# Expert results turned by VectorE and scattered as quarter rows, in an attention and mixture-of-experts kernel

## The chip, the cores and the metric

The kernel runs on one core of a Trainium2 chip, as one launch. The metric is the device time of one execution in microseconds. Engines are named as in the profile: PE (TensorE), PEld (its weight loads), DVE (VectorE), ACT (ScalarE), POOL (GpSimd) and SP (the queue that issues most DMAs).

## The reference

Two layers. The first is a gated linear attention over 4 batches, 8 heads, 768 steps and 48 columns per head. Its output, 3072 tokens of 384 columns, goes through a mixture of 8 experts, of which each token uses the one with the highest logit:

```python
f = 1.0 / (1.0 + np.exp(-f_logit))
for t in range(S):
    state = f[:, :, t, :, None] * state + np.einsum('bhd,bhe->bhde', k[:, :, t], v[:, :, t])
    y[:, :, t] = np.einsum('bhd,bhde->bhe', q[:, :, t], state)
x = y.transpose(0, 2, 1, 3).reshape(B * S, H * D)             # 3072 x 384
e_idx = np.argmax(x @ w_gate, axis=1)
gate_w = softmax(x @ w_gate)[np.arange(N), e_idx]
eom = 1.0 / (1.0 + np.exp(-(x @ w_output_gate)))
for e in range(E):                                             # 8 experts
    mask = e_idx == e
    ye = np.maximum(x[mask] @ w1[e], 0.0) @ w2[e]              # 384 -> 1024 -> 384
    out[mask] = gate_w[mask, None] * eom[mask, e, None] * ye
```

## The kernel before

**Attention and routing.** The attention works in 24 chunks of 128 tokens. Each chunk's rows, with 384 columns, the token's number and 2 x 8 logits behind them (`RW` = 401 numbers), are scattered by POOL into `xs_dram`, where each expert has its own slots. These scatters are declared independent of each other.

**The experts in order of size.** `Experts.run` goes through the stages s = 0 to 7. The largest expert comes first, and stage s makes room for `CAPS[s]` tokens: 512, 448, 432, 416, 400, 400, 384, 376. A stage has two halves. The first product (`mm1`, eight steps f of nine matmuls, L782) gives h, with columns for tokens; ACT and DVE split it into a high and a low part (`hh` L786, `hl` L787). The second product (`mm2`, eight steps of nine matmuls, L804) gives y in three PSUM tiles of 128 columns of the model each. Every operand is split into a high and a low part, so that each product is three matmuls. Stage 0 does half of its work early, while the last attention chunk ends.

**What runs beside PE.** In the first half `split` makes the high (ACT, L657) and low (DVE, L658) parts of w2. In the second half the list `front` holds, for the next expert, the four splits of w1 and three `x_in` (a DVE turn L743, an ACT cast L749, a DVE subtraction L750); one of them is taken at each step f. In stage 0 the three `x_in` come ahead of the remaining splits. The gain operations (`gain_ops`, 13 of them on DVE, ACT and POOL, L719 to L733) make each token's factor `k.gain` and its row number `k.dst`; up to two are taken at each step, for the next expert, in the second half.

**How results leave.** For experts of over 384 slots (s = 0 to 5) `y_out` copies the three PSUM tiles to SBUF at the end of the stage (L829). In the next stage, at steps f = 1 to 4 of the first product, `put` turns 128 tokens at a time back with three PE transposes (L835), ACT scales them (L838) and POOL scatters 128 rows of 384 columns to `out` (L843). The two smallest experts (s = 6, 7) use `mm2_rows` (L818), which gives rows directly.

**Order.** `chain` fixes each of DVE, ACT, POOL and PE to the order in which the program writes its instructions. SP issues DMAs in program order as well: `load` issues w1 of the next expert, `load_rest` its tokens (`tokens_in`, four loads L686 of 32 partitions and one, L690, of the 17 numbers behind each row, 68 B) and then w2 (L647). `load(1)` and `load_rest(1)` stand at the beginning of `run`, ahead of stage 0's second product. `first_m` holds these numbers for s = 0; it is loaded in two parts with that expert's early and late tokens.

Of the kernel before, what the change touches and what calls it, by code (L numbers as in the profile page):

```python
# [26 lines left out]
TS = 128  # L27
# [12 lines left out]
QW = KC * BL  # L40
NTC = N // C
# [7 lines left out]
HELD = 256  # L49

# [546 lines left out]
class Experts:  # L597
# [4 lines left out]
    def __init__(self, tc, nc, k, r, raw, right, w1, w2, xs_dram, out, kp):  # L602
        self.tc, self.nc, self.k, self.r, self.raw, self.right, self.kp = tc, nc, k, r, raw, right, kp
        self.w1, self.w2, self.xs, self.out = w1, w2, xs_dram.rearrange("(e n) w -> e n w", e=E), out
        k.gain = kp.tile([TS, NT, E], F32, name="gain")
        k.dst = kp.tile([TS, NT, E], I32, name="dst")

        self.first = kp.tile([128, SLOTS // BL, QW], F32, name="first_x")
        self.first_m = kp.tile([TS, NT, RW - DM], F32, name="first_m")
        self.apart, self.cleared, self.number = [], [], {}  # L610
        self.wr, self.whl, self.todo, self.gq = {}, {}, [], []
        self.xq, self.xt, self.hs, self.ys, self.ysb = {}, {}, {}, {}, {}
# [11 lines left out]
    def open_rest(self, ctx):  # L624
        pool = lambda name, bufs, **kw: ctx.enter_context(self.tc.tile_pool(name=name, bufs=bufs, **kw))
        self.xp, self.hp, self.yp = pool("mo_x", 2), pool("mo_h", 9), pool("mo_y", 1)
        self.psy, self.pso = pool("mo_psy", 1, space=PSUM), pool("mo_pso", 1, space=PSUM)
        self.yt = [self.yp.tile([128, SLOTS], F32, name=f"y{d}") for d in range(KC)]
# [22 lines left out]
    def split(self, m, s, i, eng=None):  # L651
        flat = lambda a: a.rearrange("p a b -> p (a b)")
# [4 lines left out]
        self.nc.scalar.copy(out=flat(hi), in_=flat(t))  # L657
        (eng or self.nc.vector).tensor_tensor(out=flat(lo), in0=flat(t), in1=flat(hi.bitcast(F32)), op=ALU.subtract)  # L658
# [17 lines left out]
    def tokens_in(self, s, j0, j1):  # L676
# [4 lines left out]
        if s == 0:  # L681
            t, m = self.first, self.first_m
        else:
            t, m = (self.xp.tile([128, SLOTS // BL, QW], F32, name="xq"),
                    self.xp.tile([TS, NT, RW - DM], F32, name="xm"))
# [4 lines left out]
        loads.append(self.nc.sync.dma_start(  # L690
            out=m[:, j0:j1, :], in_=self.xs[e, j0 * TS:j1 * TS, DM:RW].rearrange("o (j p) w -> p (o j) w", p=TS)))
# [6 lines left out]
        else:  # L698
            self.meta = getattr(self, "meta", []) + [(s, 0, j1, m)]
        self.xq[s] = t  # L700

    def gains(self):

        kp = self.kp
        for s, j0, j1, t in self.meta:
            n = j1 - j0
            d, up, dn = (kp.tile([128, NT, E], F32, name=m)[:, 0:n] for m in ("g_d", "g_up", "g_dn"))
            mx, sm, so = (kp.tile([128, NT], F32, name=m)[:, 0:n] for m in ("g_mx", "g_sm", "g_so"))
            self.gq += self.gain_ops(s, j0, j1, t, d, up, dn, mx, sm, so)
        self.meta = []  # L710

    def gain_ops(self, s, j0, j1, t, d, up, dn, mx, sm, so):
        nc, k = self.nc, self.k
        tt, red, act = nc.vector.tensor_tensor, nc.vector.tensor_reduce, nc.scalar.activation
        sig, n = AF.Sigmoid, j1 - j0
        lg, og = t[:, 0:n, 1:1 + E], t[:, 0:n, 1 + E:1 + 2 * E]
        mine = k.perm[:, s, :] if s > 0 else self.r.top
        return [
            lambda: nc.gpsimd.tensor_scalar(out=k.dst[:, j0:j1, s], in0=t[:, 0:n, 0], scalar1=0.0,  # L719
                                            scalar2=float(BIG), op0=ALU.max, op1=ALU.min),  # L720
            lambda: red(out=mx, in_=lg, axis=AX.X, op=ALU.max),
            lambda: tt(out=d, in0=lg, in1=mx.unsqueeze(2).broadcast_to([128, n, E]), op=ALU.subtract),

            lambda: (act(out=up, in_=d, func=sig), act(out=dn, in_=d, func=sig, scale=-1.0)),
            lambda: tt(out=d, in0=og, in1=mine.unsqueeze(1).broadcast_to([128, n, E]), op=ALU.mult),
            lambda: red(out=so, in_=d, axis=AX.X, op=ALU.add),
            lambda: act(out=so, in_=so, func=sig),
            lambda: nc.vector.reciprocal(out=dn, in_=dn),
            lambda: tt(out=up, in0=up, in1=dn, op=ALU.mult),
            lambda: red(out=sm, in_=up, axis=AX.X, op=ALU.add),  # L730
            lambda: nc.vector.tensor_scalar(out=sm, in0=sm, scalar1=1e-9, scalar2=None, op0=ALU.add),
            lambda: nc.vector.reciprocal(out=sm, in_=sm),
            lambda: tt(out=k.gain[:, j0:j1, s], in0=sm, in1=so, op=ALU.mult),  # L733
# [60 lines left out]
    def mm2(self, s, f, part=0):  # L794
# [4 lines left out]
        for d in range(KC):  # L799
            if f == 0 and part == 0:  # L800
                self.ys[d] = self.psy.tile([128, 512], F32, name=f"y_ps{d}")
            ds = slice(d * 128, d * 128 + 128)
            for i, (a, b) in enumerate(((wh, hh), (wl, hh), (wh, hl))):
                self.nc.tensor.matmul(self.ys[d][:, c0:c0 + n], a[:, f % 2, ds], b,  # L804
# [3 lines left out]
    def mm2_rows(self, s, step):  # L808

        k, nc = self.k, self.nc  # L810
        for j, n in self.rows(s):
            ps = self.psy.tile([128, 512], F32, name=f"y_ps{j}")
# [11 lines left out]

    def y_out(self, s):
        for d in range(KC):
            t = self.yt[d]
            copy = self.nc.vector.tensor_copy if d == 1 else self.nc.scalar.copy
            copy(out=t[:, 0:CAPS[s]], in_=self.ys[d][:, 0:CAPS[s]])  # L829
            self.ysb[s, d] = t  # L830

    def put(self, s, j, n):
        ps = self.pso.tile([128, KC, 128], F32, name="o_ps")
        for d in range(KC):
            self.nc.tensor.transpose(out=ps[:, d, :], in_=self.ysb[s, d][:, j * TS:j * TS + TS],  # L835
                                     identity=self.k.ident)
        t = self.yp.tile([TS, DM], F32, name="o", bufs=3)
# [316 lines left out]
```

## Time and profile before

| | |
|---|---|
| median of 3 runs | 360.17 us (360.13 to 360.51) |
| profiled execution | 360.28 us |
| its span in the trace | 358.5 us |
| granted clock over the span | 0.998 |

The span runs from the first to the last instruction of the program in the trace; 1.78 us of the profiled execution lie around it. Times below are in microseconds from the span's start, unless they are in ns.

### The profile page before, as it was taken

To read this page: it belongs to the slowest core of one execution; us is meant where nothing else is said; L and a number is where in the kernel's file an instruction comes from. 1 tells how busy PE (TensorE), PEld (TensorE's weight loads), DVE (VectorE), ACT (ScalarE), POOL (GpSimd) and SP (SyncE) were. 2 spreads that over 40 slices of the span, in tenths; PEclk is the share of its full clock that TensorE was granted. 3 is DMA by queue.
4 is the path that set the end of the run, shared out by engine and by line. 5 is a ranking of instruction groups with operands and counts; after the bars stand their busy time and mean duration, and the time that the engine had idled before them with its cause. 6 is when DMAs were issued, how large, how long until landed. Compare 5 with 4: busy or idle time off the path is not lost.

```text
span 358.5 us, 8438 instructions
## 1 busy us (share of the span) xinstructions
PE 346.2 (97%) x3109; PEld 324.2 (90%) x3109; DVE 245.3 (68%) x510; ACT 198.1 (55%) x468; POOL 144.4 (40%) x183
## 2 busy tenths in 40 slices
PE   7899999999999899999999999999999999999992
PEld 2678898988988899999999999999999999999992
DVE  6998989898996775785764774583684584475600
ACT  3476776776766652566535645644654654654510
POOL 8586789899989850002112201210210310232011
PEclk9999999999999999999999999999999999999999
DMA  7999999999527935968674456356555555421001
GB/s 256 350 359 354 346 257 271 295 269 261 197 66 254 284 109 155 278 193 189 190 187 99 159 182 141 135 181 137 180 179 117 181 181 123 169 91 39 0 25 45
DMA packets 66117, 67.11 MB, mean 187 GB/s; under 512 B 22019, under 2 KB 60694, under 8 KB 66065
## 3 DMA queue, kind: packets, MB, share of 16 engines
q1 hardware_dynamic: 62752, 56.82, 57.2%
q0 software_dynamic: 3312, 9.65, 7.4%
q8 instruction: 26, 0.43, 0.5%
q14 instruction: 27, 0.21, 0.2%
HBM read 53.53 MB, written 13.39 MB: 187 GB/s over the span
## 4 chain that ended last, share of the span: by engine, by line
PE 88%; DVE 4%; DMA 3%; ACT 2%; issue 2%; POOL 0%; POOLq 0%; ACTq 0%; DVEq 0%
PE h_ps L782 31%; PE y_ps L804 24%; PE x_ps L336 6%; PE a_ps L248 5%; PE y_ps L818 5%; PE two_ps L316 3%; PE two_ps L308 3%; PE one_ps L316 3%; PE kn_ps L265 3%; PE one_ps L281 2%; PE o_ps L835 2%; DMA out<-o,dst 1%; DVE p L212 1%; DVE i L219 1%; DMA f_t<-in_f 1%
## 5 line engine op out<-in xcount | busy, mean ns | idle before, releaser
L843 POOL DMA_INDIRECT out<-o,dst x30 | 30.5, 1015 | 171.2 <-ACT o L838 97.5
L787 DVE SCALAR_TENSOR_TENSOR hl<-h_ps,hh 128x256 fp32r<-128x256 f32 (+6 forms) x72 | 39.3, 546 | 49.2 <-ACT hh L786 48.9
L782 PE MATMUL h_ps<-xh,w1h 128*128 128x400 f32 (+6 forms) x192 | 67.1, 349 | 0.0
L782 PE MATMUL h_ps<-xh,w1l 128*128 128x400 f32 (+6 forms) x192 | 65.1, 339 | 0.0
L782 PE MATMUL h_ps<-xl,w1h 128*128 128x400 f32 (+6 forms) x192 | 65.0, 339 | 0.0
L786 ACT ACTIVATE hh<-h_ps 128x256 fp32r<-128x256 f32 (+6 forms) x72 | 34.8, 484 | 47.8 <-PE h_ps L782 46.8
L804 PE MATMUL y_ps<-hh,w2h 128*128 128x256 f32 (+4 forms) x168 | 55.7, 332 | 0.0
L804 PE MATMUL y_ps<-hh,w2l 128*128 128x256 f32 (+4 forms) x168 | 55.6, 331 | 0.0
L804 PE MATMUL y_ps<-hl,w2h 128*128 128x256 f32 (+4 forms) x168 | 55.6, 331 | 0.0
L782 PEld LDWEIGHTS h_ps<-xl,w1h 128*128 128x128 f32 x192 | 36.1, 188 | 0.4
L782 PEld LDWEIGHTS h_ps<-xh,w1l 128*128 128x128 f32 x192 | 36.0, 188 | 0.5
L782 PEld LDWEIGHTS h_ps<-xh,w1h 128*128 128x128 f32 x192 | 36.1, 188 | 0.4
L658 DVE TENSOR_TENSOR w2l<-w2r,w2h 128x768 fp32r<-128x768 f32 x31 | 29.7, 958 | 4.2 <-ACT w2h L657 2.0
L226 POOL TENSOR_TENSOR q_t<-q_t,p 128x512 f32<-128x512 f32 x24 | 30.6, 1275 | 4.6 <-DVE p L212 4.4
L804 PEld LDWEIGHTS y_ps<-hh,w2h 128*128 128x128 f32 x168 | 31.6, 188 | 0.4
L804 PEld LDWEIGHTS y_ps<-hl,w2h 128*128 128x128 f32 x168 | 31.6, 188 | 0.4
L804 PEld LDWEIGHTS y_ps<-hh,w2l 128*128 128x128 f32 x168 | 31.6, 188 | 0.4
L212 DVE TENSOR_TENSOR_SCAN p<-f_ps,start_p 128x511 f32<-128x511 f32 x22 | 28.0, 1274 | 3.7 <-ACT start_p L200 2.0
L248 PE MATMUL a_ps<-q_t,k_t 64*128 64x128 f32 x384 | 28.3, 285 | 2.2 <-ACT kn L273 1.4
L658 DVE TENSOR_TENSOR w1l<-w1r,w1h 128x768 fp32r<-128x768 f32 x29 | 27.8, 958 | 3.7 <-ACT w1h L657 3.0
L749 ACT CAST xh<-xr 128x400 fp32r<-128x400 f32 (+6 forms) x24 | 12.2, 518 | 31.7 <-DVE xr L743 31.6
L223 POOL TENSOR_TENSOR k_t<-k_t,i 128x512 f32<-128x512 f32 x21 | 26.9, 1282 | 3.6 <-DVE i L219 2.6
(168 smaller groups left out, 741.8 us busy)
## 6 DMA issues: line engine op xcount, KB each, us to landing
w1r<-in_w SPq DMA_DIRECT2D x32, 384.0 KB, 3.9
w2r<-in_w SPq DMA_DIRECT2D x32, 384.0 KB, 3.2
v_t<-in_v SPq DMA_DIRECT2D x12, 512.0 KB, 9.3
xs_dram<-empty SPq DMA_DIRECT2D x8, 401.0 KB, 10.6
f_t<-in_f SPq DMA_DIRECT2D x6, 512.0 KB
q_t<-in_q SPq DMA_DIRECT2D x6, 512.0 KB
k_t<-in_k SPq DMA_DIRECT2D x6, 512.0 KB, 9.6
f_t<-in_f SPq DMA_DIRECT2D x12, 192.0 KB, 8.7
```

Of the source, the lines that this page charges most:

```text
L212: nc.vector.tensor_tensor_scan(out=flat(d["p"])[:, 1:n], data0=flat(d["f"])[:, 0:n - 1], data1=sp[:, 1:n], initial=sp[:, 0:1], op0=ALU.mul ...
L223: eng.tensor_tensor(out=k_t[i][:, :, sl], in0=k_t[i][:, :, sl], in1=d["i"], op=ALU.mult)
L226: nc.gpsimd.tensor_tensor(out=q_t[i][:, :, sl], in0=q_t[i][:, :, sl], in1=d["p"], op=ALU.mult)
L248: nc.tensor.matmul(aps[t][par][:, g, :], k_t[b % 2][r, g, sl], q_t[b % 2][r, g, sl], start=(g == 0), stop=(g == NP - 1))
L316: nc.tensor.matmul(yps[t][g % 2][r0:r0 + 64, g // 2, :], v_t[b][:, c, 64 * h:64 * h + 64], at[t][:, h % 2, g, :], start=((first or c == 0) ...
L336: nc.tensor.matmul(xps[t][:, g, :], xt[t][:, g, :], turn[:, g, :], start=(g == 0), stop=(g == NP - 1))
L658: (eng or self.nc.vector).tensor_tensor(out=flat(lo), in0=flat(t), in1=flat(hi.bitcast(F32)), op=ALU.subtract)
L782: nc.tensor.matmul(ps[:, 0:n], a[:, c, cs], b, start=(i == 0), stop=(i == 3 * KC - 1))
L786: nc.scalar.activation(out=hi, in_=ps[:, 0:n], func=AF.Relu)
L787: nc.vector.scalar_tensor_tensor(out=lo, in0=ps[:, 0:n], scalar=0.0, in1=hi.bitcast(F32), op0=ALU.max, op1=ALU.subtract)
L804: self.nc.tensor.matmul(self.ys[d][:, c0:c0 + n], a[:, f % 2, ds], b, start=(f == 0 and i == 0 and part == 0), stop=(f == KF - 1 and i == ...
L843: self.nc.gpsimd.indirect_dma_start(out=self.out, out_offset=bass.IndirectOffsetOnAxis(ap=self.k.dst[0:n, j, s:s + 1], axis=0), in_=t[0:n] ...
```

## The change

- `y_out` uses three DVE transposes of 32x32 blocks, straight from PSUM, into a tile with two buffers. Columns of w2 are permuted in `split`, so that after this turn partition 32q + i holds quarter q (96 columns) of token i of a block of 32. The PE transposes, the tile `o_ps` and the copies of y are gone.
- `put` now takes a block of 32 tokens: ACT scales 128x96 in place, and POOL scatters 128 quarter rows. For s = 0 to 5 that is 16, 14, 14, 13, 13 and 13 blocks. They start at step f = 5 of the next stage's first product, two a step, and go on through its second product.
- All scatters to `out` are declared independent of each other.
- The 17 numbers behind each row are loaded by `meta_in`: for s = 0 to 5 in four loads, one to each 32 partitions, so that each quarter row has its own scale and row number. `meta_in(0)` stands at the beginning of `run`, after `load(1)` and ahead of `load_rest(1)`; the others stand after their expert's tokens.
- `gains(s)` runs in stage s: in the first product for s > 0, in the second product for s = 0. It uses Exp in place of Sigmoid, and one ACT operation fewer.
- The count in `check` uses an `h_ps` buffer.

```diff
+TURNED = sum(c > KC * 128 for c in CAPS)
+HOLD = 5
...
+        self.ys = [self.psy.tile([128, 512], F32, name=f"y_ps{d}") for d in range(KC)]
...
     def load_rest(self, s):
             self.tokens_in(s, 0, len(self.rows(s)))
+            self.meta_in(s)
...
     def split(self, m, s, i, eng=None):
+        if m == 2 and s < TURNED:
+            to = lambda a: a.rearrange("p a b -> p (a b)").rearrange("p (c x i) -> p x c i", c=KC, i=BL)
+            of = lambda a: a.rearrange("p a (q c i) -> p (a q) c i", c=KC, i=BL)
...
-        self.nc.scalar.copy(out=flat(hi), in_=flat(t))
+        self.nc.scalar.copy(out=to(hi), in_=of(t))
...
-        loads.append(self.nc.sync.dma_start(
-            out=m[:, j0:j1, :], in_=self.xs[e, j0 * TS:j1 * TS, DM:RW].rearrange("o (j p) w -> p (o j) w", p=TS)))
...
+    def meta_in(self, s):
+        e, nb = bass.ds(self.number[s], 1), self.blocks(s)
+        m = self.xp.tile([128, SLOTS // BL, RW - DM], F32, name="xm")
+        if s < TURNED:
+            for q in range(NQ):
+                self.nc.sync.dma_start(
+                    out=m[BL * q:BL * q + BL, 0:nb, :],
+                    in_=self.xs[e, 0:BL * nb, DM:RW].rearrange("o (a j) w -> j (o a) w", j=BL))
+            self.meta[s] = (nb, m)
...
+            lambda: act(out=up, in_=d, func=AF.Exp),
...
+            lambda: act(out=so, in_=so, func=AF.Exp, scale=-1.0),
...
+    def blocks(self, s):
+        return -(-CAPS[s] // BL)
+
     def y_out(self, s):
+        nb = self.blocks(s)
+        t = self.ysb[s] = self.yp.tile([128, SLOTS // BL, QW], F32, name="yr", bufs=2)
         for d in range(KC):
-            t = self.yt[d]
-            copy = self.nc.vector.tensor_copy if d == 1 else self.nc.scalar.copy
-            copy(out=t[:, 0:CAPS[s]], in_=self.ys[d][:, 0:CAPS[s]])
-            self.ysb[s, d] = t
-
-    def put(self, s, j, n):
-        ps = self.pso.tile([128, KC, 128], F32, name="o_ps")
-        for d in range(KC):
-            self.nc.tensor.transpose(out=ps[:, d, :], in_=self.ysb[s, d][:, j * TS:j * TS + TS],
-                                     identity=self.k.ident)
-        t = self.yp.tile([TS, DM], F32, name="o", bufs=3)
-        self.nc.scalar.activation(out=t[0:n], in_=ps[0:n].rearrange("p a b -> p (a b)"), func=AF.Copy,
-                                  scale=self.k.gain[0:n, j, s:s + 1])
-        self.scatter(s, j, n, t)
+            self.nc.vector.transpose(out=t[:, 0:nb, BL * d:BL * d + BL], in_=self.ys[d][:, 0:BL * nb])
+
+    def put(self, s, a):
+        t = self.ysb[s][:, a, :]
+        self.nc.scalar.activation(out=t, in_=t, func=AF.Copy, scale=self.k.gain[:, a, s:s + 1])
+        self.other_rows(self.nc.gpsimd.indirect_dma_start(
+            out=self.out.rearrange("n (q w) -> (n q) w", q=NQ),
+            out_offset=bass.IndirectOffsetOnAxis(ap=self.k.dst[:, a, s:s + 1], axis=0),
+            in_=t, in_offset=None, bounds_check=NQ * N - 1, oob_is_err=False))
+
+    def other_rows(self, i):
+        for other in self.put_out:
+            self.tc.declare_no_dep(i.ins, other.ins, reason="other tokens")
+        self.put_out.append(i)
...
     def run(self):
         step(len(self.todo))
+        self.meta_in(0)
         self.load_rest(1)
...
-            back = self.rows(s - 1) if s > 0 and len(self.rows(s - 1)) > KC else []
+            back = list(range(self.blocks(s - 1))) if 0 < s <= TURNED else []
...
+            if s > 0:
+                self.gains(s)
             for f in range(KF):
                 self.mm1(s, f)
+                self.gain(2)
...
-                if 1 <= f <= len(back):
-                    self.put(s - 1, *back[f - 1])
+                if s <= TURNED and f >= HOLD:
+                    put(2)
...
+            if s == 0:
+                self.gains(s)
...
                 if front:
                     front.pop(0)()
+                put(2)
                 self.gain(2)
```

## Rows read from the trace of the kernel before

**Rows 1.** The page, part 1: busy us (share of the span) and instructions.

```profile
PE 346.2 (97%) x3109; PEld 324.2 (90%) x3109; DVE 245.3 (68%) x510; ACT 198.1 (55%) x468; POOL 144.4 (40%) x183
```

**Rows 2.** Windows of first products, s = 1 to 6; columns: PE, PEld, DVE, ACT, POOL.

```profile
157.15:173.06 15.91, 15.91 (x85) 14.64 (x85) 9.97 (x18) 9.44 (x17) 2.51 (x2) 1.00 0.77 193
...
sum 89.11, PE 89.11 PEld 85.99 DVE 46.66 ACT 53.93 POOL 17.62; mean PE 14.85 PEld 14.33 DVE 7.78 ACT 8.99 POOL 2.94
```

**Rows 3.** Windows, second products of s = 1 to 6: the first and all six.

```profile
173.06:187.59 14.53, 14.53 (x74) 13.45 (x74) 10.77 (x30) 6.23 (x12) 2.54 (x3) 1.00 0.64 185
...
sum 80.89, PE 80.89 PEld 79.41 DVE 59.33 ACT 36.95 POOL 10.90; mean PE 13.48 PEld 13.24 DVE 9.89 ACT 6.16 POOL 1.82
```

**Rows 4.** Chain of waits: start us, us, what.

```profile
148.70 8.45 PE y_ps L804 x72
157.15 3.71 PE h_ps L782 x18
160.86 0.33 PE o_ps L835 x3
```

**Rows 5.** Groups by line and form: busy us, mean ns, idle before and releaser.

```profile
L843 POOL DMA_INDIRECT out<-o,dst x30 | 30.5, 1015 | 171.2 <-ACT o L838 97.5 <-ACT o L822 27.9 <-ACT hh L786 15.9
...
L838 ACT ACTIVATE o<-o_ps,gain 128x384 f32<-128x384 f32 x19 | 11.0, 581 | 0.0
...
L295 DVE TENSOR_TENSOR misc<-one_ps,state 128x192 f32<-128x192 f32 x16 | 5.8, 361 | 5.3 <-ACT xt L330 5.0
...
L743 DVE STREAM_TRANSPOSE xr<-xq 128x448 f32<-128x448 f32 x6 | 3.8, 635 | 0.3 <-DMA xq<-xs_dram 0.3
...
L724 ACT ACTIVATE g_up<-g_d 128x32 f32<-128x32 f32 x6 | 1.4, 230 | 6.9 <-DVE g_d L722 6.9
...
L68 ACT ACT_TABLE_LOAD x1 | 1.3, 1283 | 0.8 <-PEq L1145 0.8
...
L722 DVE TENSOR_TENSOR g_d<-xm,g_mx 128x32 f32<-128x32 f32 x5 | 0.9, 182 | 0.0
```

**Rows 6.** Waits: us in total, times, longest.

```profile
POOL out L843 <- DMA out<-o,dst: 12.7, 3, 4.8
...
DVE y L829 <- PE y_ps L804: 7.3, 5, 1.9
```

**Rows 7.** DMA issues: count, KB each, median us to landing.

```profile
w2r<-in_w SPq DMA_DIRECT2D x32, 384.0 KB, 3.2
...
out<-o,dst POOLq DMA_INDIRECT x30, 2.7
```

**Rows 8.** Timeline of POOL, scatters of the attention.

```profile
122.42 0.98 POOL L353 DMA_INDIRECT xs_dram<-xn,slot  x1 [0.30 <-issue]
123.70 1.15 POOL L353 DMA_INDIRECT xs_dram<-xn,slot  x1 [0.30 <-issue]
```

**Rows 9.** Timeline of SP, 136 to 190 us.

```profile
137.16 2.94 SPq L635 DMA_DIRECT2D w1r<-in_w  x4
140.60 3.38 SPq L686 DMA_DIRECT2D xq<-xs_dram  x4
...
145.61 2.87 SPq L647 DMA_DIRECT2D w2r<-in_w  x4
...
183.83 2.03 SPq L686 DMA_DIRECT2D xq<-xs_dram  x4
```

**Rows 10.** Timeline of DVE before the second stage.

```profile
149.93 0.65 DVE L743 STREAM_TRANSPOSE xr<-xq 128x448 f32<-128x448 f32 x1 [0.31 <-DMA xq<-xs_dram]
...
155.91 0.96 DVE L658 TENSOR_TENSOR w1l<-w1r,w1h 128x768 fp32r<-128x768 f32 x1
```

**Rows 11.** Timeline of PE, start of the second stage.

```profile
157.39 0.37 PE L782 MATMUL h_ps<-xh,w1l 128*128 128x448 f32 x1
```

**Rows 12.** DMA queues, 135 to 136 us: packets, MB, share of 16 engines.

```profile
q1 hardware_dynamic: 95, 0.01, 6.8%
```

**Rows 13.** DMA queues, 132 to 136 us.

```profile
q1 hardware_dynamic: 1360, 0.41, 46.4%
```

More of the change, by code (lines that the diff above doesn't have):

```diff
@@ L626, in open_rest @@
         self.xp, self.hp, self.yp = pool("mo_x", 2), pool("mo_h", 9), pool("mo_y", 1)
-        self.psy, self.pso = pool("mo_psy", 1, space=PSUM), pool("mo_pso", 1, space=PSUM)
-        self.yt = [self.yp.tile([128, SLOTS], F32, name=f"y{d}") for d in range(KC)]
+        self.psy = pool("mo_psy", 1, space=PSUM)
+        self.ys = [self.psy.tile([128, 512], F32, name=f"y_ps{d}") for d in range(KC)]
+        k, gp = self.k, pool("mo_g", 1)
+        k.gain = gp.tile([TS, SLOTS // BL, E], F32, name="gain")
+        k.dst = gp.tile([TS, SLOTS // BL, E], I32, name="dst")
+        self.quarter = gp.tile([128, 1], F32, name="quarter")
+        for q in range(NQ):
+            self.nc.gpsimd.memset(self.quarter[BL * q:BL * q + BL], float(q))
+        self.gp = gp
     def load(self, s, number, rest=True):
@@ L680, in tokens_in @@
         early = s == 0 and j0 == 0
[L681 to L685, printed above, removed]
+        t = self.first if s == 0 else self.xp.tile([128, SLOTS // BL, QW], F32, name="xq")
         loads = [self.nc.sync.dma_start(
@@ L713, in gain_ops, with gains @@
+    def gains(self, s):
+        kp = self.gp
+        n, t = self.meta[s]
+        d, up = (kp.tile([128, SLOTS // BL, E], F32, name=m)[:, 0:n] for m in ("g_d", "g_up"))
+        mx, sm, so = (kp.tile([128, SLOTS // BL], F32, name=m)[:, 0:n] for m in ("g_mx", "g_sm", "g_so"))
+        self.gq += self.gain_ops(s, n, t, d, up, mx, sm, so)
+    def gain_ops(self, s, n, t, d, up, mx, sm, so):
         nc, k = self.nc, self.k
-        tt, red, act = nc.vector.tensor_tensor, nc.vector.tensor_reduce, nc.scalar.activation
@@ L715, in gain_ops, with index @@
-        sig, n = AF.Sigmoid, j1 - j0
+        tt, red, act, ts = nc.vector.tensor_tensor, nc.vector.tensor_reduce, nc.scalar.activation, nc.vector.tensor_scalar
         lg, og = t[:, 0:n, 1:1 + E], t[:, 0:n, 1 + E:1 + 2 * E]
         mine = k.perm[:, s, :] if s > 0 else self.r.top
+        row = t[:, 0:n, 0]
+        def index():
+            limit = dict(scalar1=0.0, scalar2=float(BIG), op0=ALU.max, op1=ALU.min)
+            if s < TURNED:
+                nc.gpsimd.tensor_scalar(out=row, in0=row, **limit)
+                nc.gpsimd.tensor_scalar(out=k.dst[:, 0:n, s], in0=row, scalar1=float(NQ), scalar2=self.quarter,
+                                        op0=ALU.mult, op1=ALU.add)
+            else:
+                nc.gpsimd.tensor_scalar(out=k.dst[:, 0:n, s], in0=row, **limit)
@@ L811, in mm2_rows @@
         for j, n in self.rows(s):
[L812 removed]
+            ps = self.ys[j]
             i = 0
@@ L915, in run @@
                 front = []
[L916 to L920 removed]
+            if s == 0:
+                self.gains(s)
+            if s >= TURNED:
+                self.mm2_rows(s, lambda i: (front.pop(0)() if front and i % 3 == 1 else None, put(2 if i % 3 == 0 else 0)))
                 continue
@@ L946, in count @@
     def count():
-        ps = psum.tile([128, KC, 128], F32, name="o_ps")[:, 0, 0:1]
+        ps = psum.tile([128, 512], F32, name="h_ps")[:, 0:1]
         nc.tensor.matmul(ps, k.ones, okb, start=True, stop=True)
```

72 lines of the change are left out of this document (25 added, 47 removed).

## The prediction

> **What bounds the kernel now.** I read the page's busy shares first: TensorE (PE) is busy 97% of the 358.5 us span, VectorE (DVE) 68%, ScalarE (ACT) 55%, GpSimd (POOL) 40% [rows 1]. An average hides stages, so the windows come next, one for each half of a stage. [...] Last I read the chain of waits: it stays on PE, from the second products of s = 0 into the first ones of s = 1, and shows three o_ps transposes as a piece of 0.33 us between two first products [rows 4]. Those are on the path, and the change removes them.
>
> **What PE saves.** In s = 1 to 6 the first half holds 72 matmuls and the transposes of four puts, the second half 72 matmuls of the same number of columns and no transposes. The first halves sum to 89.11 us, the second to 80.89 us [rows 2, 3]. The difference, 8.22 us, is 24 puts at 0.34 us, which agrees with the piece of 0.33 us [rows 4]; by that piece it would be 7.9. I take 8.22. The profiled execution took 360.28 us (its span and 1.78 us around it); without the transposes it is 352.06 us.
>
> **What moves to VectorE.** The three copies at a stage's end (two on ACT, one on DVE) become three DVE transposes out of PSUM, which this trace does not show; the nearest row is one of 448 columns from SBUF, 0.635 us [rows 5]. Bounds: 0.6 to 1.2 us each; I take 0.65, 2 us a stage. They are hidden: at the end of the second product DVE already stands idle for PE before its copy (7.3 us in five stages) [rows 6]. With that cover gone the first hl of the stage would be late, and PE only once the three h_ps buffers are full; 3 x 1.2 us would not reach that.
>
> **What moves to ACT.** 24 scalings of 128x384 (0.581 us) go and 83 of 128x96 come (16 + 14 + 14 + 13 + 13 + 13 blocks), between the 0.230 us of a 128x32 activation and that 0.581 us [rows 5]; I take 0.33, being nearer the small one: 27 us against 14 us and the copies removed. Six of a stage fall into the last three steps of the first product, the rest into the first steps of the second, ahead of the casts that DVE needs for the next expert. There ACT is busy 6.2 us of 13.5 in the mean [rows 3], and the scale arithmetic leaves this half for the next stage's first one. DVE had 7.3 us over five stages to spare at the end of it [rows 6]; I expect about 0.5 us less in each, no stall. In the first half DVE gains nine small operations on 104 to 128 columns, between 0.182 us (32 columns) and 0.361 us (192) [rows 5]: 7.8 becomes about 10.2 us of 13.5.
>
> **What moves to POOL.** 24 scatters of up to 128 whole rows become 83 of 128 quarter rows. A scatter of whole rows takes 1.015 us [rows 5], and the attention's scatters, declared independent in the same way, start 1.28 us apart [rows 8]. 13 to 16 of them are 17 to 21 us of a stage's 27 to 30 us [rows 2, 3]. Behind a late POOL stand only its own next scatters; a result tile is needed again two stages later. I count nothing, and no gain either: POOL waited for ACT, not the other way round [rows 5]. The upper bound is the third rival.
>
> **What can stall PE: the start of the second expert.** The change puts the load of the first expert's slot numbers and logits (four issues, 2048 rows of 68 B; before, two issues of 256 rows, at earlier places) on the SP queue between the second expert's w1 and its tokens. SP issues w1 at 137.16, the tokens at 140.60 and w2 at 145.61 us, each behind the other [rows 9]. DVE waits 0.31 us for the tokens and starts the first turn at 149.93 us; the three turns end in the low part of w1, 155.91 to 156.87 us [rows 10]. The third matmul of the stage, at 157.39 us, needs that part [rows 11]. The cover is 0.5 us, so a later load goes through nearly whole. Its terms:
> - The load. Where 68 B rows went alone, 95 packets took 6.8% of 16 engines in 1 us, 11.5 ns each; where they went among token rows, 1360 packets took 46.4% in 4 us, 21.8 ns each [rows 12, 13]. 2048 of them are 1.5 to 2.8 us of all 16 engines. Against that w2, now issued later, shares less of the engines with the tokens: issued at 145.61 us and 3.2 us from landing [rows 7, 9], it had about 1 us in common with them, 0.6 us at the most. I take 1.7 us, bounds 0.9 to 2.8.
> - The gain operations between the turns work on 16 blocks, not 4: 0.5 us more, bounds 0.2 to 0.8, from the rows of 32 and 192 columns [rows 5].
> - The scales used Sigmoid and now use Exp; the trace has one table load, 1.283 us [rows 5]. A second would fall on ACT between the second cast and the third. ACT waits there for DVE anyway, some 1.5 us (the rest of one turn, one gain operation, the next turn), so it is hidden if the load may start at once, and costs 0.9 us if it waits for the Exp's operand. I take 0.4.
>
> Sum: 1.7 + 0.5 + 0.4 - 0.5 = 2.1 us, bounds 0.6 (0.9 + 0.2 + 0 - 0.5) and 4.0 (2.8 + 0.8 + 0.9 - 0.5). Late next is everything behind it: PE is full afterwards and gives nothing back. Later experts' 68 B rows stand behind their tokens, and those are early: issued at 183.83 us [rows 9], the tokens of s = 3 are used a whole first half later; w2 behind them waits for its buffers anyway. I count nothing there. The permuted w2 split has as many elements as before, in runs of 32; nothing, with 10% of its 0.96 us as upper bound, inside DVE's free time. The early loads lose one issue each, which nothing waits on.
>
> **The numbers.** 360.28 - 8.22 + 2.1 = 354.2 us for a profiled execution; the median of the runs lies 0.11 us below the profiled one, so 354.1.
>
> **The rivals.**
> - *No stall.* With w2 out of the way the tokens come as early as before; then 351.9 us, at most 352.6. For it: w2 and the tokens share the engines now. Against it: 0.5 us of cover. Chance 0.20.
> - *The table load in the open.* The Exp and its load hold ACT while DVE waits for the third cast: from rows 0.9 to 2.2 us (after the operand; or the 1.283 us again for emptying ACT) in place of 0.4, so 354.6 to 355.9 us [rows 5]. Against it: a load ahead of a waiting instruction need not wait. Chance 0.12. [...]
> - *Scatters in single file, slower.* If a scatter still waits until the one before has landed, each costs 1.0 + 2.7 us [rows 5, 7]; three times POOL did wait so, 12.7 us in all [rows 6]. POOL has from 166 us (sixth first product of s = 1) to some 13 us before the end, 180 us for 83, so it decides at 2.2 us apiece; at 3.7 us the 83 need 307 us and the kernel ends beyond 450 us. Against it: the 1.28 us [rows 8]. Chance 0.10.
> - *A larger stall.* 68 B rows go one issue after the other at the token rate, and the later stages lose their 0.5 us too: 4 to 6 us given back, 356.2 to 358.3. Chance 0.14.
> - *No gain.* DVE or ACT becomes the limit of the first half, 359.5 to 360.5 us. Against it: 10.2 of 13.5 us. Chance 0.04.
>
> My forecast, 352.7 to 355.4 us by the table load hidden, has 0.40. All but the third and the last are faster by over 0.2% (0.7 us, about what three runs that lie within 0.4 us can tell): 0.86; within 0.2% 0.04; slower 0.10. The range 351.6 to 357.8 us leaves out the slower case, no gain, and the far end of the larger stall.
>
> **What would show it.** No o_ps rows; first halves of s = 1 to 6 summing to 80.9 us plus the stall in the first; a PE gap between 157 and 160 us that DVE's w1 low part ends, with a DVE wait for xq of 1.5 to 3 us before it; 89 scatters of about 1 us, 1.3 us apart; a second table load near 154 us. I am wrong if PE waits at the start of later stages, or if scatters wait for the scatter before.

## The result and the profile after

The changed kernel took 355.24 us (median of 4 runs, 354.67 to 355.62), the kernel before 360.28 us beside it: a ratio of 0.9858 (95% interval 0.9841 to 0.9875). Forecast were 354.1 us, 351.6 to 357.8. The profiled execution took 355.4 us, its span 353.5 us against 358.5. This holds on the kind of chip on which the kernel before takes 360 us; on others, where it takes 367, the changed kernel was 11% slower, which the experiments come to. Where the runs of a kernel on one chip fall into a faster and a slower group, a ratio below is that of the faster runs, so it need not be the quotient of the medians beside it.

The page, part 1, of the changed kernel: busy us, share of the span, instructions.

```profile
PE 339.4 (96%) x3037; PEld 317.5 (90%) x3037; DVE 252.1 (71%) x514; ACT 202.6 (57%) x508; POOL 213.6 (60%) x252
```

Against [rows 1], PE has 72 matmuls fewer and is 6.8 us less busy; POOL is 69 us busier. The windows of the same halves as in [rows 2, 3] show where the time came from. Columns: length, then PE, PEld, DVE, ACT, POOL, granted clock, DMA share, GB/s. First products of s = 1 to 6:

```profile
157.15:173.38 16.23, 15.08 (x75) 13.61 (x74) 13.35 (x33) 8.90 (x20) 1.51 (x2) 1.00 0.83 198
188.16:202.33 14.17, 14.17 (x74) 13.53 (x73) 9.39 (x22) 8.08 (x17) 6.57 (x8) 1.00 0.62 143
...
sum 82.96, PE 81.81 PEld 79.53 DVE 58.05 ACT 47.92 POOL 24.92; mean PE 13.64 PEld 13.25 DVE 9.68 ACT 7.99 POOL 4.15
```

Second products of s = 1 to 6:

```profile
173.38:188.16 14.78, 14.78 (x75) 13.45 (x74) 10.42 (x21) 8.35 (x21) 11.48 (x11) 1.00 0.64 197
202.33:216.49 14.16, 14.16 (x73) 13.53 (x73) 9.62 (x14) 7.79 (x19) 10.88 (x11) 1.00 0.62 188
...
sum 81.50, PE 81.50 PEld 79.37 DVE 55.94 ACT 47.40 POOL 63.42; mean PE 13.58 PEld 13.23 DVE 9.32 ACT 7.90 POOL 10.57
```

From s = 2 on a first half is as long as a second half: the 8.22 us of transposes are gone. The first row alone has PE idle, 16.23 us with 15.08 busy. But the second halves, to which the change took nothing from PE, went from 80.89 [rows 3] to 81.50 us. So PE's matmuls are a little slower in both halves, in s = 1 to 5 (second halves: 14.53 to 14.78, 13.92 to 14.16, 13.44 to 13.68 us, and 0.06 and 0.05 more for s = 4 and 5); in s = 6 they are faster, 12.48 against 12.71 us. The sum of 0.61 has both in it.

The one gap of PE, in its timeline (start us, us, engine, line, operation; in brackets the idle time before it and what ended that):

```profile
157.58 0.37 PE L804 MATMUL h_ps<-xh,w1l 128*128 128x448 f32 x1
...
162.46 0.36 PE L804 MATMUL h_ps<-xh,w1l 128*128 128x448 f32 x1
163.97 0.47 PE L804 MATMUL h_ps<-xh,w1h 128*128 128x448 f32 x1 [1.15 <-DVE hl L809]
```

The third matmul (157.58) ran on time, and so did 24 more. The 28th started 1.51 us after the 27th, where 0.20 is usual: a stall of 1.3 us. It waits for hl of the first step, which frees the first of the three h_ps buffers. What made that hl late stands in DVE's timeline:

```profile
151.30 0.65 DVE L765 STREAM_TRANSPOSE xr<-xq 128x448 f32<-128x448 f32 x1 [1.60 <-DMA xq<-xs_dram]
...
157.73 0.95 DVE L668 TENSOR_TENSOR w1l<-w1r,w1h 128x768 fp32r<-128x768 f32 x1
158.60 0.17 DVE L750 TENSOR_SCALAR g_so<-g_so 128x16 f32<-128x16 f32 x1
159.77 0.96 DVE L668 TENSOR_TENSOR w1l<-w1r,w1h 128x768 fp32r<-128x768 f32 x1 [1.01 <-ACT w1h L667]
...
161.55 1.84 DVE L852 STREAM_TRANSPOSE yr<-y_ps 128x512 f32<-128x512 f32 x3
163.32 0.59 DVE L809 SCALAR_TENSOR_TENSOR hl<-h_ps,hh 128x448 fp32r<-128x448 f32 x1
```

The first turn is 1.37 us later than before (149.93 [rows 10]), and the low part of w1 1.82 us later (155.91 [rows 10]): 1.37 from the tokens, 0.45 mostly from wider gain operations. Then DVE waits 1.01 us for the next high part of w1, which on ACT stands behind the second Exp of the gains. Last come the three turns of `y_out`, 1.84 us ahead of hl.

SP's timeline gives the reason for the late tokens: `meta_in(0)` takes 3.67 us of issuing ahead of them, so they are issued at 144.53 instead of 140.60 us [rows 9].

```profile
140.64 3.67 SPq L709 DMA_DIRECT2D xm<-xs_dram  x4
144.53 2.74 SPq L692 DMA_DIRECT2D xq<-xs_dram  x4
```

The new operations, by line and form: busy us, mean ns, idle before and its releaser. The scatters of POOL keep their distance of 1.28 us in the timeline (178.63, 179.91).

```profile
L857 POOL DMA_INDIRECT out<-yr,dst x83 | 90.8, 1094 | 59.7 <-ACT yr L856 35.5 <-issue 10.4 <-DVE gain L755 5.3
L856 ACT ACTIVATE yr<-yr,gain 128x96 f32<-128x96 f32 x83 | 26.6, 369 | 0.0
...
L852 DVE STREAM_TRANSPOSE yr<-y_ps 128x448 f32<-128x448 f32 x6 | 3.7, 650 | 1.5 <-PE y_ps L824 1.5
```

The balance of the spans, 358.5 to 353.5: 8.22 us of transposes saved; 1.3 back in the stall; 1.35 back in the pace (second halves +0.61, first halves 82.96 - 1.3 - 80.89 = +0.77); the rest, about 0.5, lies in the last expert (s = 7) and behind it; its cause stays open.

### The profile page after: what moved, and what is told of

It reads as the page before. It is cut to its first block, busy times and chain, and to the rows that moved or that the text cites. A ratio compares the mean times of both kernels' runs of the same rounds, so it can differ in the third digit from the quotient of the medians.

```text
span 353.5 us, 8664 instructions
## 1 busy us (share of the span) xinstructions
PE 339.4 (96%) x3037; PEld 317.5 (90%) x3037; DVE 252.1 (71%) x514; ACT 202.6 (57%) x508; POOL 213.6 (60%) x252
## 3 DMA queue, kind: packets, MB, share of 16 engines
HBM read 54.04 MB, written 13.46 MB: 191 GB/s over the span
## 4 chain that ended last, share of the span: by engine, by line
PE 77%; DVE 8%; issue 4%; ACT 3%; DMA 3%; SPq 2%; POOL 1%; POOLq 0%; DVEq 0%; ACTq 0%
PE h_ps L804 27%; PE y_ps L824 20%; PE x_ps L338 6%; PE a_ps L250 5%; PE y_ps L838 5%; PE two_ps L318 3%; PE two_ps L310 3%; PE one_ps L318 3%; PE kn_ps L267 3%; PE one_ps L283 2%; DVE p L214 1%; DVE i L221 1%; SPq L709 1%; DMA xm<-xs_dram 1%; DMA f_t<-in_f 1%
## 5 line engine op out<-in xcount | busy, mean ns | idle before, releaser
L857 POOL DMA_INDIRECT out<-yr,dst x83 | 90.8, 1094 | 59.7 <-ACT yr L856 35.5
L804 PE MATMUL h_ps<-xh,w1h 128*128 128x400 f32 (+6 forms) x192 | 65.3, 340 | 1.1 <-DVE hl L809 1.1
L355 POOL DMA_INDIRECT xs_dram<-xn,slot x24 | 24.7, 1029 | 7.8 <-issue 3.8
```

The costliest lines, as they stand in the source:

```text
L355: i = nc.gpsimd.indirect_dma_start(out=xs_dram, out_offset=bass.IndirectOffsetOnAxis(ap=r.slot[:, t:t + 1], axis=0), in_=xn[t // 4][:, t % ...
L804: nc.tensor.matmul(ps[:, 0:n], a[:, c, cs], b, start=(i == 0), stop=(i == 3 * KC - 1))
L857: self.other_rows(self.nc.gpsimd.indirect_dma_start(out=self.out.rearrange("n (q w) -> (n q) w", q=NQ), out_offset=bass.IndirectOffsetOnAx ...
```

## The experiments

My theory after the result had three parts. The stall comes through the late tokens, with the three turns behind them; a rival was that the table load or the turns alone cause it. The pace goes with the program as built, not with the execution. The scatters cost nothing. The runs are from several chips; each ratio below is to the kernel before on the same chip.

**The stall, four kernels.** `again` is the changed kernel unaltered. `meta_early` moves the first expert's small rows:

```diff
 (attention, after the late tokens of s = 0)
+        ex.meta_in(0)
 (Experts.run)
-        self.meta_in(0)
 (meta_in; first_m is a new tile in kp, and the tile `ok` of the final count moves to gp)
+        m = self.first_m if s == 0 else self.xp.tile(...)
```

`exp_early` loads the table of Exp ahead of stage 0's second product, and `turn_later` puts the three turns behind the next stage's first step:

```diff
 (exp_early, in run)
+        self.nc.scalar.activation(out=self.quarter_e, in_=self.quarter, func=AF.Exp)
 (turn_later, in run)
+                if f == 0 and 0 < s <= TURNED:
+                    self.y_out(s - 1)
-            self.y_out(s)
```

> The changed kernel once more, unaltered, on another occasion. Both theories: 354.7 to 355.6 us, the spread of its runs so far. What it tells is the pace of the matmuls: in the profile of the change 72 matmuls of 448 columns took 14.78 us and in the kernel before 14.53 us (0.2053 against 0.2018 us each), and such differences add up to about 1.3 us. If the pace belongs to the program, this profile shows 14.78 us again, stage by stage; if it belongs to the occasion, another number, and the time moves with it.

> The first expert's slot numbers and logits are loaded right behind its late tokens, before the second expert's w1, into a tile of their own. Theory (late tokens put DVE behind, and PE stalls once the three h_ps buffers are full): the tokens are waited for 0.3 us and not 1.6, DVE's work before the second stage ends 1.3 us earlier, and the stall of 1.2 to 1.5 us near 163 us shrinks to 0.0 to 0.3 us: 353.8 to 354.2 us. Rival (the delay comes from the wider gain operations, the table load and the three turns at the stage's end, whatever the tokens do): no less than 355.0 us.

> One small Exp is put on ACT ahead of stage 0's second product, where ACT stands idle, so that the second table load falls there. By the trace of the change the load held up the third cast by 0.1 us only, since ACT waits there for DVE: 355.0 to 355.3 us, 0 to 0.2 us less. Rival (the table load of 1.28 us is what DVE lacks before the second stage): 1.0 to 1.3 us less, 353.9 to 354.2 us.

> The three turns out of PSUM stand behind the first step of the next stage's first product, instead of at the end of the stage. Theory (they stand ahead of the hl that frees the first h_ps buffer): that hl of the second stage comes 1.8 us earlier, PE finds the buffer free, and the stall of 1.2 to 1.5 us is gone although the tokens are as late as in the change: 353.7 to 354.2 us. In the other stages nothing moves. Rival (PE waits because the tokens and weights are late, and the order on DVE does not matter): 355.0 us or more.

These four went to a chip where the kernel before took 367.08 us. There `again` took 406.83 us (ratio 1.1089, 1.106 to 1.1118), `meta_early` 411.66 (1.1175), `exp_early` 406.48 (1.1082) and `turn_later` 399.1 (390.74 to 402.94). Their times tell of something else (below), but the first product of s = 1 is undisturbed in each, and its windows answer the question. In turn: `again`, `exp_early`, `turn_later`.

```profile
164.36:180.68 16.32, 14.89 (x75) 13.42 (x73) 13.45 (x33) 8.90 (x20) 1.35 (x2) 1.00 0.82 192
```

```profile
164.45:180.79 16.34, 14.89 (x74) 13.43 (x73) 13.41 (x33) 8.90 (x20) 1.35 (x2) 1.00 0.81 187
```

```profile
164.19:180.15 15.96, 14.94 (x75) 13.42 (x73) 13.08 (x32) 8.69 (x20) 1.16 (x1) 1.00 0.85 198
```

An earlier table load changes nothing: 16.34 against 16.32 us. In `turn_later` PE still idles 1.0 us, one step later: the turns now stand ahead of the second hl instead of the first, so this run did not take them out of PE's way, and it doesn't tell how much of the stall is theirs. `meta_early` has 14.87 us there, without a gap. Where the tokens' wait differed by chance, the gap differed with it: 1.60 us of DVE waiting for xq and 1.15 us of PE in the changed kernel, 0.82 and 0.4 us in `half_put`, 1.93 and 1.5 us in `no_drain`, none and none in `meta_half` (all below; of these kernels only `meta_half` differs from the changed one ahead of this place). First `half_put`, then `no_drain`, then the hl of `meta_half`:

```profile
150.79 0.65 DVE L765 STREAM_TRANSPOSE xr<-xq 128x448 f32<-128x448 f32 x1 [0.82 <-DMA xq<-xs_dram]
PE h_ps L804 <- DVE hl L809: 0.4, 1, 0.4
152.43 0.65 DVE L765 STREAM_TRANSPOSE xr<-xq 128x448 f32<-128x448 f32 x1 [1.93 <-DMA xq<-xs_dram]
PE h_ps L804 <- DVE hl L809: 1.5, 1, 1.5
161.90 0.59 DVE L811 SCALAR_TENSOR_TENSOR hl<-h_ps,hh 128x448 fp32r<-128x448 f32 x1
```

So the small rows on SP's queue started it. With them early, hl(0) of `meta_half` starts at 161.90 us, still behind three turns and the same 1.01 us wait for ACT, and PE does not wait. `placed` (below), which has the tiles of `meta_early` but not its earlier load, keeps the stall, so the tiles are not what removed it.

**The scatters and the drain, and the transposes alone.** `half_put` drops the scatters of odd blocks, `no_drain` POOL's drain ahead of each stage from s = 2 on; `no_turn` is the kernel before without PE's transposes; `before_2` is the kernel before.

```diff
 (half_put, in put behind the scale)
+        if a % 2:
+            return
 (no_drain, in run)
-            if s > 1:
-                self.nc.gpsimd.drain()
 (no_turn, against the kernel before)
-        for d in range(KC):
-            self.nc.tensor.transpose(out=ps[:, d, :], in_=self.ysb[s, d][:, j * TS:j * TS + TS], ...)
-        self.nc.scalar.activation(out=t[0:n], in_=ps[0:n].rearrange("p a b -> p (a b)"), ...)
+        self.nc.scalar.activation(out=t[0:n], in_=self.ysb[s, j % KC][0:n, 0:DM], ...)
```

> The changed kernel without POOL's DRAIN ahead of the stages from s=2 on; all else stands. In the unaltered run of the first batch on a chip where the kernel before takes 367 us, the changed kernel took 406.8: in the second products of s=1 to 5, PE waited for nothing that the profile shows while POOL's DRAIN of 9 to 11.5 us stood behind running scatters and SP's register moves took 0.7 us each. Theory A (a drain behind running scatters slows every engine's sequencer): without it the slow stretches go and the time is 0.98 to 0.99 of the kernel before, whatever chip it is. Theory B (scatters beside small loads slow them, drain or not): where the kernel before takes about 367 us the time stays 1.08 to 1.12 of it. Where the kernel before takes about 360 us both say 355 (0.986), and the run tells only what the drain itself costs there: nothing.

> The changed kernel with the quarter-row scatters of the odd blocks left out (41 or so of 83 scatters are gone, half of those experts' results are not stored), scales and turns stand. POOL is then done with an expert's scatters some 20 us earlier, and the drain of the next stage finds them finished. Theory A (drain behind running scatters) and theory C (too many scatters at once): no slow stretch, 0.98 to 0.985 of the kernel before on any chip. Theory B (any scatter beside the loads of w1 and tokens): slow stretches stay, about half as long, 1.03 to 1.07 where the kernel before takes about 367 us. On a chip where that takes 360 us: 354.5 to 355.4, since the scatters are on no path that sets the end but the tail's.

> The kernel before with TensorE's transposes in the puts left out (ScalarE scales and POOL scatters the unturned result: what is stored is not turned back), nothing else of the change. This is the first term of my sum alone: 24 puts of 4 transposes, 8.2 us of TensorE, so 0.975 to 0.979 of the kernel before (351.6 to 352.3 where that takes 360.3), with no stall at the start of s=1. If the unexplained 1.4 us of the changed kernel come with the changed layout of the weights or the scatters, this kernel's second-product matmuls of 448 columns take 0.202 us as before; if they come with PE that never rests, they take 0.205 here too and the ratio is 0.979 to 0.982.

> The kernel before, for its profile on this chip. Where it takes about 367 us, theory A (drain behind running scatters) says its drains of 3 to 4 us show short slow stretches of SP's register moves and of PE (6 to 7 us in all); theory B says they lie where scatters and small loads run together; a third reading, that the whole chip is slower by its memory, says longer waits for DMA and no slow moves.

Here the kernel before took 360.54 us (`before_2` 360.37). `half_put` took 356.01 us (0.9876, 0.986 to 0.9892), as long as the changed kernel: 40 scatters fewer save nothing, so on this chip they are hidden. `no_drain` surprised: 364.66 us (1.0118, 1.0095 to 1.0142), where I had said the drain costs nothing. Its last scatter starts at 348.76 us and its span ends at 363.0; in the changed kernel these are 347.54 and 353.5. So without drains in the stages some 8 us more stand behind the last scatter, in the open. Where the drains stand in the changed kernel they are hidden: no half from s = 2 on has PE waiting (from 157 to 327 us its view of waits has one wait of PE, the 1.1 us for hl at s = 1).

`no_turn` took 353.83 us (0.9815, 0.9799 to 0.9831), less gain than forecast, and with no stall (a put has three transposes, not four as its expectation says: 72 in 24 puts). Its windows, first and second product of s = 1, then of s = 2, and the first of s = 3:

```profile
157.63:172.50 14.87, 14.87 (x74) 13.47 (x73) 10.80 (x21) 10.64 (x19) 2.05 (x2) 1.00 0.82 206
172.50:187.49 14.99, 14.99 (x75) 13.41 (x73) 10.72 (x30) 6.23 (x12) 2.30 (x3) 1.00 0.66 183
187.49:201.89 14.40, 14.40 (x74) 13.46 (x72) 7.65 (x12) 9.20 (x16) 2.86 (x3) 1.00 0.48 125
201.89:216.29 14.40, 14.40 (x74) 13.46 (x72) 9.89 (x23) 6.17 (x12) 2.11 (x3) 1.00 0.66 185
216.29:229.75 13.46, 13.46 (x73) 13.44 (x72) 7.43 (x12) 8.93 (x16) 2.27 (x3) 1.00 0.50 133
```

The second product of s = 1 was 14.53 us before [rows 3], 14.78 in the changed kernel, and is 14.99 here: 72 matmuls of 448 columns at 202, 205 and 208 ns, at the same granted clock and with PE always busy. So a slower pace can come without quarter rows and without turns on DVE. Nor is it that PE never rests, which stood as a rival in the expectation: at 416 columns PE is as busy here, and its pace is that of the kernel before (13.46 us, against 13.44 in the second product there), not that of the changed kernel (13.67).

**The pace.** `placed` is the changed kernel with one unused tile more and the tile `ok` moved, as `meta_early` has them; no step moves.

```diff
+        self.pad = kp.tile([128, SLOTS // BL, RW - DM], F32, name="pad")
+        nc.gpsimd.memset(self.pad[:, 0, 0:1], 0.0)
...
-    ok = pool.tile([128, NTC * NP], F32, name="ok")
+    ok = k.gp.tile([128, NTC * NP], F32, name="ok")
```

> The kernel meta_early once more, for its time where the kernel before takes about 360 us: the small rows (row numbers and logits) of the first expert are loaded right behind its late tokens, some 5 us of SP's queue earlier, and the tokens of s=1 follow w1 at once; a 128x16x17 tile more stands in the pool of constants for them. In its first run (on the chip where the kernel before takes 367 us) the first product of s=1 took 14.87 us instead of 16.3, and the undisturbed halves of later stages took 13.92 (432 columns), 13.45 (416), 13.12 (400) and 12.37 (376), the paces of the kernel before, not 14.16, 13.68, 13.20 and 12.48 as in the changed kernel. Theory (stall through the late tokens, and a matmul pace that goes with where the tiles lie): both terms gone, 355.2 - 1.4 - 1.3 = 352.5, 0.977 to 0.980 of the kernel before. Rival 1 (the stall comes from the three turns and gain operations, wherever the load stands): the stall stays, 353.5 to 354.2. Rival 2 (the slower pace goes with turns and quarter rows): 353.8, paces of 14.16, 13.68 and 13.20.

> The changed kernel with nothing but the placement of tiles as in meta_early: an unused 128x16x17 tile in the pool of constants, and the 128-row tile of the final count in the small pool. No load and no step is moved. Theory (the pace of the matmuls goes with where the tiles lie in SBUF): the stall of 1.45 us at s=1 stays, the halves of 432, 416 and 400 columns take 13.92, 13.44 and 13.12 to 13.15 us instead of 14.16, 13.68 and 13.20, and the time is 355.2 - 1.3 = 353.9 (0.981 to 0.984 of the kernel before). Rival (the pace goes with what is issued, not with where it lies): paces of the changed kernel, 355.2 (0.9845 to 0.987).

This chip was again of the other kind (367.86 us before): `meta_early` a second time 412.68 us (1.1085, 1.1046 to 1.1123), `placed` 414.98 (404.72 to 416.65). The undisturbed first products tell. `placed`, for 448, 416, 400 and 400 columns:

```profile
165.04:180.93 15.89, 14.83 (x74) 13.42 (x73) 13.02 (x33) 8.61 (x20) 1.21 (x2) 1.00 0.77 201
242.87:256.34 13.47, 13.47 (x74) 13.45 (x72) 9.14 (x22) 7.71 (x17) 1.79 (x2) 1.00 0.29 88
279.23:292.37 13.14, 13.14 (x73) 13.14 (x72) 8.73 (x21) 7.53 (x16) 1.72 (x2) 1.00 0.30 88
314.29:327.44 13.15, 13.15 (x74) 13.15 (x73) 8.94 (x22) 7.56 (x16) 1.74 (x2) 1.00 0.29 87
```

The same 400 columns in `again`, on the chip of the first four runs:

```profile
277.39:290.59 13.20, 13.20 (x74) 13.20 (x73) 8.95 (x22) 7.58 (x16) 1.75 (x2) 1.00 0.30 88
312.30:325.50 13.20, 13.20 (x73) 13.20 (x73) 8.94 (x22) 7.59 (x16) 1.75 (x2) 1.00 0.29 89
```

The changed kernel has 13.20 on both chips, and an unused tile and a moved one turn it into 13.14 (and 416 columns from 13.67 into 13.47, the pace before, with turns and quarter rows in place); the stall stays. The pace goes with the program as built. That it is the place of the tiles in SBUF, as I expected, is not borne out: `no_turn` moves no tile there that I know of and has a third pace, and `meta_drain` (below), which differs from `meta_early` in nothing but the place of POOL's drain, takes 14.40 us for the 432 columns of s = 2, where `meta_early` takes 13.93 (`meta_early` a second time and `meta_half`, on two more chips, 13.92). `meta_early`, then `meta_drain`:

```profile
206.21:220.14 13.93, 13.93 (x74) 13.52 (x72) 9.18 (x22) 7.87 (x17) 1.90 (x2) 1.00 0.28 87
204.91:219.31 14.40, 14.40 (x73) 13.46 (x72) 9.44 (x22) 7.92 (x17) 2.01 (x2) 1.00 0.28 86
```

What in the build sets the pace stays open.

**The other kind of chip.** On three chips (367 to 368 us before) the changed kernel and its variants took 399 to 418 us. Of the 52 us that `again` loses against the changed kernel's first profile, 7.2 lie ahead of s = 1, which starts at 164.36 us and not at 157.15; the kernel before loses 7 us on these chips as well, but no trace of it from one of them was kept. The rest is lost later. In `again` the second products of s = 1 to 5 take 21.6 to 22.5 us instead of 13.2 to 14.8. Windows of the first of them:

```profile
188.00:192.00 4.00, 4.00 (x22) 3.51 (x21) 2.78 (x6) 1.87 (x5) 3.09 (x4) 1.00 0.53 175
192.00:196.00 4.00, 2.50 (x11) 1.68 (x9) 0.00 (x0) 0.00 (x0) 3.09 (x4) 1.00 0.67 176
196.00:200.00 4.00, 2.09 (x5) 1.06 (x5) 0.00 (x0) 0.00 (x0) 3.09 (x4) 0.70 0.93 165
200.00:204.00 4.00, 2.98 (x7) 2.19 (x8) 0.94 (x3) 0.55 (x1) 0.47 (x1) 0.50 0.10 8
```

PE goes from 22 matmuls in 4 us to 11 and 5, while DVE and ACT idle and POOL scatters on. The granted clock is still 1.00 from 192 to 196 us, where PE is busy for 2.50 of 4.00 us, and falls only behind that, to 0.70 and 0.50: PE slows before its clock does. The view of waits names nothing that PE waits for:

```profile
PE y_ps L824 <- issue: 25.6, 31, 1.8
```

A rival is that PE's next instructions were fetched too slowly. The trace speaks against it: from 189 to 197 us, in the second half of which PE is already slow, the view of DMA lists these two queues (packets, MB, share of 16 engines) and no packet of an instruction queue:

```profile
q1 hardware_dynamic: 1970, 1.22, 57.6%
q0 software_dynamic: 162, 0.24, 10.3%
```

Scatters and the drain behind them seemed to set the place, so `meta_drain` is `meta_early` with the drain moved to where the scatters are over:

```diff
-            if s > 1:
-                self.nc.gpsimd.drain()
...
             for f in range(KF):
+                if s > 1 and f == 3:
+                    self.nc.gpsimd.drain()
                 self.mm1(s, f)
```

> The kernel meta_early with POOL's drain of each stage from s=2 on moved behind the third first product of the stage, where the scatters of the stage before are over, so that no drain waits behind running scatters. On a chip where the kernel before takes about 360 us: stall gone (1.2 us) and pace of the kernel before (1.3 to 1.4 us), so 352.5 to 353 (0.977 to 0.981); rival, that the drain's own 4 to 5 us now push the scatters of a stage past its end and into the tail: 354 to 358. On a chip where the kernel before takes about 367 us: if a drain that waits behind scatters is what slows the sequencers, the second products of s=1 to 5 lose their 8 to 10 us each and the time is 358 to 362 (0.975 to 0.985); if scatters beside the loads do it, drain or not, it stays at 405 to 415 (1.10 to 1.13).

It took 418.1 us (408.18 to 418.23; 367.26 before), with the slow stretch in the same place, ahead of the drain:

```profile
184.00:188.00 4.00, 4.00 (x22) 3.61 (x21) 2.33 (x6) 2.79 (x7) 3.14 (x3) 1.00 0.64 212
188.00:192.00 4.00, 2.60 (x11) 1.67 (x9) 1.83 (x3) 1.40 (x4) 3.03 (x4) 1.00 0.46 141
192.00:196.00 4.00, 1.35 (x3) 0.58 (x3) 0.00 (x0) 0.00 (x0) 3.09 (x4) 0.71 0.91 250
```

So a drain behind running scatters is not the cause. `turn_later` has scatters beside the loads in 233 to 238 us with PE at full pace, and in 264 to 268 us not:

```profile
233.00:238.00 5.00, 5.00 (x28) 4.91 (x27) 0.00 (x0) 0.00 (x0) 3.46 (x4) 1.00 1.13 200
...
264.00:268.00 4.00, 2.92 (x12) 1.79 (x11) 0.00 (x0) 0.00 (x0) 3.09 (x4) 1.00 1.25 195
```

The first of the two is no exception, though: there another engine was late. The first product of s = 3 begins at 233.86 us, but ACT's first operation on it only at 238.71, 4.85 us later; in the changed kernel on the first chip it follows 1.74 us behind (216.49 to 218.23). So it is not PE alone that slows. `turn_later`, then the changed kernel:

```profile
238.71 0.52 ACT L808 ACTIVATE hh<-h_ps 128x416 fp32r<-128x416 f32 x1 [7.50 <-PE h_ps L804]
218.23 0.52 ACT L808 ACTIVATE hh<-h_ps 128x416 fp32r<-128x416 f32 x1 [4.56 <-PE h_ps L804]
```

The slow stretches lie where quarter rows are scattered while the next expert's w1 and tokens come in (in `again` w1 is issued from 183.69 us on and the tokens from 192.74, scatters start until 199.50, and PE is slow from about 193 to 202). That the scatters are the cause is argued from this, not shown; why only on some chips, and what holds PE there, stays open. `meta_half`, `meta_early` with half of its scatters, was to tell whether each scatter pays.

```diff
 (meta_early, in put behind the scale)
+        if a % 2:
+            return
```

> The kernel meta_early with the quarter-row scatters of the odd blocks left out (half of the results of those experts are not stored); turns and scales stand. On a chip where the kernel before takes about 360 us, where half_put took the time of the changed kernel (356.0, 0.9876): the stall and the slower pace are gone and scatters cost nothing, 352.8 to 353.8, 0.979 to 0.982. On a chip where the kernel before takes about 367 us, where meta_early took 1.11 to 1.12 of it: if the slow stretches of PE are paid by the scatter (each of the 83 adds its share of some 50 us), 41 of them gone leave 380 to 392 us (1.04 to 1.07); if the small loads of rows and tokens, which stand as they were, are what slows PE, it stays at 1.10 to 1.12; if scatters slow PE only once they reach into the loads of the next expert's w1 and tokens, half of them are over before these and the time is 355 to 362 (0.97 to 0.985).

It went to a chip of the first kind: 353.65 us (0.9804, 0.9786 to 0.9821; 360.75 before). So the question for the other kind was not answered; but it shows `meta_early`'s PE side where the change does help. Products of s = 1, and the first of s = 2:

```profile
157.37:172.25 14.88, 14.88 (x75) 13.47 (x74) 11.96 (x28) 8.66 (x19) 1.16 (x1) 1.00 0.82 202
172.25:187.13 14.88, 14.88 (x75) 13.42 (x73) 10.32 (x21) 8.48 (x21) 7.99 (x9) 1.00 0.60 185
187.13:201.05 13.92, 13.92 (x74) 13.52 (x72) 9.31 (x22) 7.87 (x17) 1.07 (x1) 1.00 0.56 126
```

No stall, and 13.92 us for s = 2 where the changed kernel has 14.17; the 448 columns of s = 1, at 14.88 us, are slower than there (14.78) and than before (14.53). Against `half_put` it gains 2.4 us. `meta_early` with all its scatters was not timed on such a chip; from `half_put`, where half of them changed nothing, about 353.5 us is my estimate for it.

## Why the prediction was right, and where not

- **What PE saves: right.** Before, PE was busy throughout the halves of s = 1 to 6, for 89.11 of 89.11 us and 80.89 of 80.89 [rows 2, 3], so what it no longer does there comes off the time. The first halves lost their transposes in full, and the first halves from s = 2 on equal the second ones.
- **The pace: a term that was missing.** I took the remaining matmuls at their old duration. They cost 1.35 us more in s = 1 to 6; `no_turn`, `placed` and `meta_drain` show that this goes with the build; neither turns and quarter rows nor the place of tiles accounts for it alone. No row of before could have told it, but the paces of 202 to 208 ns for one shape are the width to allow for it.
- **The stall at the second expert: the place and the cause right, the path and size off.** The forecast was 2.1 us, from 1.7 of load, 0.5 of wider gain operations and 0.4 of table load, less 0.5 of cover; it was 1.3 in the profiled execution (0.4 and 1.5 us of waiting in two kernels with the same order at this place). The tokens came 1.37 us later, and the other two terms were 0.45 together. The step that failed is "The third matmul of the stage, at 157.39 us, needs that part": the low part in question serves a later step of f, and PE ran 27 matmuls without it. The cover was not that matmul's 0.5 us but that of three h_ps buffers: PE idles from 162.8 to 164.0 us, behind hl, and not between 157 and 160 behind the low part, as the signs had it. With the terms as measured the forecast's sum, 1.37 + 0.45 - 0.5, gives the 1.3 us that came; that is luck, since it takes the wrong path.
- **"They are hidden": failed for s = 0.** The turns took about the 0.65 us each that I gave them (0.617 to 0.665), but I argued that three of them could not use up the h_ps buffers. With the tokens early they do not (`meta_half`); behind late tokens, wider gain operations and the wait for ACT they are the last 1.84 us ahead of hl. That wait, 1.01 us, I had not seen: the Exp of g_so stands ahead of a high part on ACT and waits for DVE.
- **ACT: right in effect.** A scale took 0.369 us, not 0.33; no half from s = 2 on shows PE waiting.
- **The table load: hidden, as forecast.** It starts at 154.57 us, takes 1.28, and the Exp follows at 155.87; the third cast starts at 156.09, 0.1 us after its operand. No time for emptying ACT shows beside it: 0.02 us lie between load and Exp, 0.01 between the load and the cast ahead of it, and `exp_early` gains nothing (its first product of s = 1 took 16.34 us, that of `again` 16.32).
- **POOL: no cost on the one kind of chip** (1.28 us apart, `half_put`), so the rival of single file is out there. On the other kind the change costs 11%, and there the whole verdict turns. No rival of the prediction has this, and "I count nothing" cannot be relied on there, though no run shows that it is the scatters.
- **The sum.** Stall 0.8 us smaller, pace 1.35 and end 0.5 larger than forecast: 1.1 us above the 354.1. The terms were less good than the total: an error on one side met two on the other, and the range was wide enough to hold "no stall" as well.

## What to carry to other kernels

Follow a late operand to the first instruction that truly reads it, and through the buffers between, before calling a matmul the victim; then sum all that now stands ahead of the instruction which frees the buffer. Small loads of many short rows do not belong on a queue right ahead of what the critical path reads next: here four of them took 3.67 us of issuing, and the tokens behind them came 1.37 us later; an earlier place, in front of the next weights, cost no wait of PE (`meta_half`). Put on PE's sum an allowance for its pace, some 1% (here 1.35 us on the 161.8 of the twelve halves), even when its remaining instructions do not change, and time a change that trades PE for many scatters on more than one chip (here a ratio of 0.986 on one kind and 1.109 on the other).

## What the runs showed of the hardware

- One shape of matmul took several steady paces (202, 205, 207, 208 ns for 448 columns in the kernel before, the changed kernel, `meta_half` and `no_turn`; 193, 197, 200 for 432) at the same granted clock, 1.00. They repeated on another chip for one program (400 columns: 13.20 us a half in the changed kernel on two chips), and small changes elsewhere in it moved them (`placed`: 13.14 and 13.15; `meta_drain`: 14.40 for 432 columns, against 13.93 in `meta_early`).
- POOL's drains from s = 2 on cost PE no wait in the changed kernel (one wait of PE from 157 to 327 us, 1.1 us at s = 1), and without them some 8 us more lay at the end: the span ends 14.2 us after the start of the last scatter in `no_drain`, 6.0 in the changed kernel.
- On three chips out of at least five PE slowed, from 22 matmuls in 4 us to 11, 5 and 7 (`again`, 192 to 204 us) and to 11 and 3 (`meta_drain`), while scatters and loads ran together. The profile names nothing that it waited for: 25.6, 28.8 and, in `placed`, 24.8 us of waits at the second products have no releaser. On the others the changed kernel and its variants have no such waits.
